# A new order for the first chunk's work, work moved between engines, and blockwise turns on VectorE for three groups

## The chip, the cores and the metric

The kernel runs on one core of a Trainium2 chip. Its engines are TensorE (PE in the rows; PEld is its weight load), VectorE (DVE), ScalarE (ACT), GpSimd (POOL) and SyncE (SP), which here only issues DMAs. The metric is device microseconds of one execution, the median over runs.

## The reference, cut to what matters

Attention comes first: 4 batches, 8 heads of width 64, 768 tokens. Each query sees a local window (distance under 16) and 24 summaries of 32 tokens each: the maximum of the keys and the mean of the values. Then a two-layer network (512 to 2048 to 512, with ELU) runs on all 3072 tokens.

```
k_sum = k.reshape(B, H, nb, block, D).max(axis=3)
v_sum = v.reshape(B, H, nb, block, D).mean(axis=3)
scores_l = scale * np.matmul(q, k.transpose(0, 1, 3, 2))      # kept where |i - j| < 16
scores_s = scale * np.einsum('bhsd,bhnd->bhsn', q, k_sum) + np.log(block)
a = softmax over the concatenation of both
x = matmul(a, concatenate([v, v_sum], axis=2)), heads side by side
h = x @ w_in
g = np.where(h > 0.0, h, np.exp(np.minimum(h, 0.0)) - 1.0)
out = (g @ w_out).astype(np.float32)
```

All inputs are float32 except the weights w_in and w_out, which are float64.

## The kernel before, in words

The network runs over six chunks of 512 tokens. A chunk has 16 hidden slices f of 128. For each slice, layer 1 is 12 matmuls of 128x512 and layer 2 another 12: every operand is split into a high fp32r part and the rest, and three of the four products are kept. That makes 24 matmuls per slice, 384 per chunk and 2304 in all.

The first chunk is special, for it also brings in the weights. Each of the 32 weight blocks (16 of w_in, 16 of w_out) arrives as float64 bits and is converted by five steps: `X` (low bits, POOL), `M` (exponent, ACT, into PSUM), `S` (two joins, DVE), `H` (the high fp32r part, a cast) and `L` (the rest, a subtraction). Also in the first chunk stand the attention of its own 512 tokens (four head pairs, words `sl`, `ss`, `low`, `exp`, `z`, `norm`, `tr`, `ptc`, `val`) and the attention of the second chunk, in groups 0 to 3 of two head pairs each (`gsc`, `glow`, `ge`, `gz`, `gn`, `gtr`, `gpc`, `gval`, `gxh`, `gxl`). ELU is `E` (exponential, ACT) with two more steps, and `G` and `gl` split the result for layer 2. `L1h`, `L1l`, `L2a`, `L2b`, `L2c` are the matmuls; `w`, `kq`, `ve`, `vo`, `q`, `K`, `sk`, `sv`, `vm` issue DMAs on SP; `idle` and `warm` are matmuls on zeros.

The order of all this is written out by hand in the table `FIRST`: a word is a step with its numbers, and each engine executes its own steps strictly in the order of the table. Nothing reorders them later. Chunks 2 to 6 come from a loop (L792 on), whose order a scheduler settles for ACT, DVE and POOL; there the probabilities of a group are turned by `group_blocks`, 16 block transposes on DVE (L580), in place of TensorE's transposes (L199) and a copy out of PSUM (L569).

Buffers matter at a few places. Scores of pair 0 and 3 share two PSUM banks; the turned probabilities of the first chunk all use the two buffers of the bank tag `h`, which layer 1 uses too. The weight tiles lend their space to the first chunk's keys, queries and probabilities, so some weight loads wait for attention steps.

Of the kernel before, what the change touches and what calls it, by code (L numbers as in the profile page):

```python
# [38 lines left out]

FIRST = """  # L40
    kq.2 ve kq.3 vo max.0 sl.0 max.1 ss.0 sl.1 low.0.1 ss.1 idle.2.180 low.0.0 exp.0.1 low.1.0 sums.0 low.1.1
    exp.0.0 sl.2 idle.2.120 w.0 max.2 exp.1.1 z.0 ss.2 w.1 norm.0.1 sums.1 low.2.1 exp.1.0 norm.0.0 tr.0.1
    low.2.0 warm.1.180 q.0 sums.2 ptc.0.1.0 w.2 exp.2.1 z.1 sl.3 max.3 norm.1.0 w.3 exp.2.0 spr.3.0 ss.3
    warm.1.300 norm.1.1 spr.0.0 spr.2.0 low.3.1 w.4 mv.0.2.0 mv.0.0.1 low.3.0 mv.1.0.0 exp.3.1 spr.1.0 mv.1.3.0
    z.2 tr.0.0 warm.1.480 mv.1.1.0 tr.1.1 warm.1.480 ptc.0.0.0 exp.3.0 norm.2.0 sk.0 ptc.1.1.0 norm.2.1 tr.2.0
    q.1 mv.0.1.1 z.3 ptc.2.0.1 X.0 w.5 tr.2.1 mv.1.2.1 X.1 tr.1.0 ptc.2.1.1 val.0 norm.3.0 ptc.1.0.0 M.0 M.1 S.0
    norm.3.1 val.1 mv.0.3.1 xh.0 w.6 X.2 S.1 tr.3.0 xh.1 X.3 tr.3.1 ptc.3.0.1 sk.1 val.2 ptc.3.1.1 xl.0 H.0.1
    w.7 xl.1 val.3 xh.2 H.1.1 X.4 xl.2 L.0 w.8 first.0 xh.3 M.2 xl.3 L.1 first.1 M.3 sk.2 S.2 first.2 w.9
    first.3 S.3 H.2.1 M.4 L1h.1 E.0 L.2 w.10 ts.0 H.3 Y.5 stt.0 L.3 L1l.1 sk.3 S.4 G.0 E.1 gl.0 L2a.0 w.11 M.5
    L2c.0 M.6 Y.6 S.5 H.4 w.12 L2b.0 X.7 ts.1 H.5 L.4 L1h.2 sv.0 M.7 stt.1 L.5 w.13 G.1 S.6 L1l.2 gl.1 S.7 L2a.1  # L50
    H.6 w.14 L2c.1 L.6 H.7 sv.1 L2b.1 E.2 ks.3 L.7 K.2 vl vm.0 vm.1 gsc.0 ts.2 X.8 stt.2 L1h.3 X.9 glow.0.0 G.2
    X.10 glow.0.1 M.8 gl.2 ge.0.0 L1l.3 S.8 q.2 L2a.2 w.15 X.11 E.3 gz.0.0 X.12 L2c.2 H.8 ts.3 w.16 M.9 L.8
    L2b.2 stt.3 M.10 S.9 L1h.4 G.3 sv.2 gn.0.0 ge.0.1 S.10 gl.3 L1l.4 gz.0.1 L2a.3 E.4 gn.0.1 M.11 ts.4 L2c.3
    H.9 stt.4 H.10 L2b.3 L.9 vs.1 G.4 gtr.0.0 L.10 L1h.5 S.11 gl.4 ks.2 H.11 L1l.5 gpc.0.0.1 ks.0 L.11 M.12
    gtr.0.1 ks.1 L2a.4 gpc.0.1.1 X.13 M.13 S.12 L2b.4 X.14 E.5 L2c.4 pm.2 S.13 H.12 pm.3 gval.0 X.15 X.16 ts.5
    H.13 gsc.1 w.17 w.18 sv.3 L.12 stt.5 w.19 G.5 L1h.6 glow.1.0 L.13 gxh.0 glow.1.1 M.14 w.20 gl.5 gxl.0 L1l.6
    M.15 ge.1.0 S.14 w.21 L2a.5 L2b.5 S.15 E.6 gap.6 w.22 H.14 L2c.5 X.17 H.15 L.14 L1h.7 w.23 M.16 gz.1.0
    larger.6 M.17 L.15 S.16 w.24 G.6 L1l.7 ge.1.1 gl.6 L2a.6 S.17 K.3 E.7 gap.7 X.18 L2b.6 H.16 gz.1.1 gn.1.0
    L2c.6 L.16 larger.7 gtr.1.0 vs.2 L1h.8 G.7 q.3 gn.1.1 H.17 vs.0 w.25 gpc.1.0.1 gl.7 vs.3 M.18 L1l.8 S.18
    w.26 gtr.1.1 E.8 X.19 L2a.7 gpc.1.1.1 L.17 ts.8 M.19 w.27 L2b.7 stt.8 X.20 L2c.7 S.19 G.8 X.21 w.28 gval.1  # L60
    gl.8 w.29 gsc.2 gxh.1 X.22 H.18 gxl.1 H.19 L1h.9 L.18 glow.2.0 w.30 M.20 L.19 w.31 ge.2.0 L1l.9 S.20 X.23
    L2a.8 glow.2.1 E.9 X.24 L2b.8 H.20 ts.9 ge.2.1 L.20 L2c.8 stt.9 gz.2.0 mmul G.9 L1h.10 gz.2.1 mact mm gl.9
    M.21 M.22 S.21 L1l.10 gn.2.0 L2a.9 gn.2.1 S.22 M.23 E.10 L2b.9 X.25 H.21 ts.10 X.26 L2c.9 H.22 stt.10 L.21
    gtr.2.0 G.10 L1h.11 gpc.2.0.1 L.22 S.23 M.24 L1l.11 gl.10 S.24 H.23 gtr.2.1 L.23 L2a.10 gpc.2.1.0 H.24
    L2b.10 M.25 L.24 E.11 S.25 L2c.10 X.27 gval.2 K.4 q.4 ts.11 X.28 H.25 stt.11 L.25 gsc.3 G.11 gxh.2 L1h.12
    gl.11 glow.3.1 glow.3.0 ge.3.1 gxl.2 X.29 L1l.12 X.30 M.26 L2a.11 gz.3.1 E.12 gn.3.1 S.26 L2b.11 ge.3.0
    L2c.11 ts.12 H.26 stt.12 L1h.13 M.27 L.26 G.12 S.27 M.28 gl.12 L1l.13 gz.3.0 M.29 L2a.12 S.28 gn.3.0 E.13
    H.27 L2b.12 X.31 ts.13 H.28 L2c.12 L.27 stt.13 gtr.3.0 L.28 L1h.14 S.29 gpc.3.0.1 M.30 G.13 S.30 L1l.14 H.29
    gl.13 gtr.3.1 L2a.13 L.29 gpc.3.1.1 M.31 L2b.13 H.30 S.31 L2c.13 E.14 L.30 gval.3 ts.14 stt.14 gsc.4 gxh.3
    H.31 gxl.3 G.14 L1h.15 L.31 glow.4.0 ge.4.0 gl.14 L1l.15 L2a.14 E.15 ts.15 L2b.14 stt.15 L2c.14 glow.4.1  # L70
    G.15 gl.15 ge.4.1 gz.4.0 gz.4.1 gn.4.0 gn.4.1
# [806 lines left out]
```

## Time and profile before

| | us |
|---|---|
| median of 3 runs | 611.12 (610.88 to 611.23) |
| span of the profiled execution | 1539.6 |
| first matmul of layer 1 in the profiled execution | 55.0 |
| first matmul of the second chunk in the profiled execution | 302.4 |

The profiled execution's span is 2.5 times the time of the runs, and no time beside that span is given for it. So the profile is not a picture of a timed run: it must be read engine by engine, and the prediction says how. Durations stand at the right of each group of rows (busy, mean ns of one); a bracket in a timeline row is the idle time of the engine just before, and what ended it.

### The profile page before, as it was taken

To read this page: it belongs to the slowest core of one execution; us is meant where nothing else is said; L and a number is where in the kernel's file an instruction comes from. 1 tells how busy PE (TensorE), PEld (TensorE's weight loads), DVE (VectorE), ACT (ScalarE), POOL (GpSimd) and SP (SyncE) were. 2 spreads that over 40 slices of the span, in tenths; PEclk is the share of its full clock that TensorE was granted. 3 is DMA by queue.
4 is the path that set the end of the run, shared out by engine and by line. 5 is a ranking of instruction groups with operands and counts; after the bars stand their busy time and mean duration, and the time that the engine had idled before them with its cause. 6 is when DMAs were issued, how large, how long until landed. Compare 5 with 4: busy or idle time off the path is not lost.

```text
span 1539.6 us, 11202 instructions
## 1 busy us (share of the span) xinstructions
PE 1534.8 (100%) x4123; PEld 931.8 (61%) x4123; DVE 364.7 (24%) x1063; ACT 271.8 (18%) x762; POOL 243.2 (16%) x280
## 2 busy tenths in 40 slices
...
GB/s 294 158 109 82 55 51 35 27 28 27 1 53 25 47 71 28 0 26 1 47 47 37 41 7 43 28 1 54 27 0 17 1 0 0 27 0 0 0 0 27
DMA packets 63551, 58.62 MB, mean 38 GB/s; under 512 B 22649, under 2 KB 54905, under 8 KB 63497
## 3 DMA queue, kind: packets, MB, share of 16 engines
q1 hardware_dynamic: 60184, 52.02, 11.0%
...
## 4 chain that ended last, share of the span: by engine, by line
PE 100%; ACT 0%; DVE 0%; issue 0%
PE o L696 38%; PE h L635 37%; PE h L646 7%; PE o L686 7%; PE o_ps L599 3%; PE s L542 3%; PE t_ps L199 1%; PE idle L275 1%; PE s L355 1%; PE o_ps L382 1%; PE h L426 0%; PE vsps L401 0%; PE vsps L512 0%; ACT ots L723 0%; DVE kw L265 0%
## 5 line engine op out<-in xcount | busy, mean ns | idle before, releaser
L635 PE MATMUL h<-xh,w 128*128 128x512 f32 x640 | 472.6, 825 | 0.0
L696 PE MATMUL o<-w,gh 128*128 128x512 f32 x648 | 407.9, 827 | 0.0
L696 PEld LDWEIGHTS o<-w,gh 128*128 128x128 f32 x648 | 225.2, 348 | 160.3 <-issue 160.1
L635 PEld LDWEIGHTS h<-xh,w 128*128 128x128 f32 x640 | 224.1, 350 | 161.2 <-issue 160.1
L676 POOL TENSOR_TENSOR gl<-e,gh 128x512 fp32r<-128x512 f32 x96 | 122.4, 1275 | 944.0 <-ACT gh L671 844.3
L635 PE MATMUL h<-xl,w 128*128 128x512 f32 x320 | 265.9, 831 | 0.0
L655 DVE TENSOR_SCALAR e<-e 128x512 f32<-128x512 f32 x94 | 41.3, 439 | 844.7 <-ACT e L651 844.7
L696 PE MATMUL o<-w,gl 128*128 128x512 f32 x324 | 218.1, 832 | 0.0
L651 ACT ACTIVATE e<-h 128x512 f32<-128x512 f32 x96 | 57.4, 598 | 873.9 <-PE h L635 801.1
L696 PEld LDWEIGHTS o<-w,gl 128*128 128x128 f32 x324 | 115.8, 358 | 73.6 <-issue 71.8
L635 PEld LDWEIGHTS h<-xl,w 128*128 128x128 f32 x320 | 112.3, 351 | 65.5 <-issue 65.5
L580 DVE STREAM_TRANSPOSE pt<-sm 32x256 f32<-32x256 f32 x256 | 111.4, 435 | 4.1
L646 PE MATMUL h<-xh,w 128*128 128x512 f32 x120 | 90.3, 837 | 0.0
L181 ACT ACTIVATE sm<-sm,mx 128x120 f32<-128x120 f32 x160 | 61.5, 388 | 111.5 <-DVE mx L173 111.5
L686 PE MATMUL o<-w,gh 128*128 128x512 f32 x120 | 78.4, 832 | 0.0
L671 ACT CAST gh<-e 128x512 fp32r<-128x512 f32 x96 | 59.5, 620 | 100.9 <-DVE e L666 94.4
L173 DVE CUSTOM_DVE_ANT_0 sm<-s,mask 128x120 f32<-128x120 f32 x160 | 34.2, 279 | 135.3 <-PE s L542 135.3
L666 DVE SCALAR_TENSOR_TENSOR e<-h,e 128x512 f32<-128x512 f32 x94 | 65.0, 692 | 3.2
L190 POOL TENSOR_TENSOR sm<-sm,z 128x480 f32<-128x480 f32 x40 | 38.8, 988 | 139.4 <-DVE z L193 132.1
L646 PEld LDWEIGHTS h<-xh,w 128*128 128x128 f32 x120 | 42.2, 352 | 28.9 <-issue 27.1
L161 POOL TENSOR_TENSOR w<-cv,w 128x512 fp32r<-128x512 f32 x32 | 40.7, 1286 | 119.9 <-ACT w L158 119.7
L686 PEld LDWEIGHTS o<-w,gh 128*128 128x128 f32 x120 | 41.6, 349 | 27.6 <-issue 27.0
...
## 6 DMA issues: line engine op xcount, KB each, us to landing
...
```

Source lines behind the costliest of these rows:

```text
L181: nc.scalar.activation(out=sm[:, t, :], in_=sm[:, t, :], func=AF.Exp, bias=mx[:, t, :], scale=-1.0, accum_out=z[:, t, :])
L542: nc.tensor.matmul(s_of[g, h][half, 2 * i + t // 2, cols], q_t[rows, i, t * QW:(t + 1) * QW], right, start=True, stop=True)
L580: nc.vector.transpose(out=dst[k, :, q], in_=src[q, :, k])
L599: nc.tensor.matmul(o_of[g][cols, i, t * QW:(t + 1) * QW], left, pt[0:KC, h, 2 * i + t // 2, t % 2 * QW:(t % 2 + 1) * QW], start=True, stop ...
L635: nc.tensor.matmul(h_ps, w[:, a, cols], bb[:, cc, :], start=(k == 0), stop=(k == 3 * NCC - 1))
L646: nc.tensor.matmul(h_ps, w[:, lo, cc * P:(cc + 1) * P], bb[:, cc, :], start=(lo, cc, i) == (0, 0, 0), stop=(lo, cc) == (1, NCC - 1))
L651: nc.scalar.activation(out=e, in_=h_ps, func=AF.Exp)
L666: top = nc.vector.scalar_tensor_tensor(out=e, in0=h_ps, scalar=0.0, in1=e, op0=ALU.max, op1=ALU.add)
L671: nc.scalar.copy(out=gh, in_=e)
L676: nc.gpsimd.tensor_tensor(out=gl, in0=e, in1=gs[(c, f)][0].bitcast(F32), op=ALU.subtract)
L686: nc.tensor.matmul(o_acc[0][s], gs[(0, f)][a][:, s * P:(s + 1) * P], w[:, bb, :], start=(f, part) == (0, 0), stop=False)
L696: nc.tensor.matmul(o_acc[c][s], a[:, s * P:(s + 1) * P], w[:, bb, :], start=first and f == 0, stop=last and f == NF - 1)
```

## The change

The table `FIRST` is replaced by another order of nearly the same words. The words also choose other engines or other forms:

| word | before | after |
|---|---|---|
| `L`, rest of a weight | 32 on POOL | 22 on POOL, 10 on DVE |
| `H`, high part of a weight | 29 on ACT, 3 on POOL | 15 on ACT, 17 on POOL |
| `G`, high part of ELU | 16 on ACT | 6 on ACT, 10 on POOL |
| `gl`, rest of ELU | 16 on POOL | 15 on POOL, 1 on DVE |
| ELU after `E` | 14 `ts`+`stt` (DVE, DVE), 2 `gap`+`larger` (ACT, DVE) | 16 `gap`+`larger` |
| `norm` and `gn`, row scaling | 18 on POOL | 12 on POOL, 6 on DVE |
| `mv`, means to value tiles | 4 on POOL, 4 on ACT | 7 on POOL, 1 on ACT |
| `gtr`, four PE transposes each | 8 | 2 (group 0 alone) |
| `gpc`, copy out of PSUM | 7 on ACT, 1 on DVE | 2 on ACT |
| `gb`, four block transposes on DVE each | 0 | 12 (groups 1 to 3) |
| `ptc`, copy out of PSUM | 4 on ACT, 4 on DVE | 5 on ACT, 3 on DVE |
| `idle`, `warm` | 2, 4 | 0, 2 |

`ve` becomes four words, one for each part of its loads, and `tr` takes a bank (seven single banks beside `h`). Words that the table does not use (`zh`, `pb`, `ew`, `rs`, `dm`) are defined as well.

```
+BLOCKS_FROM = 1
 FIRST = """
-    kq.2 ve kq.3 vo max.0 sl.0 max.1 ss.0 sl.1 low.0.1 ss.1 idle.2.180 low.0.0 exp.0.1 low.1.0 sums.0 low.1.1
...
+    max.0 sl.0 ss.0 low.0.1 exp.0.1 max.1 low.0.0 exp.0.0 sl.1 ss.1 ve.2 kq.2 sl.2 low.1.1 exp.1.1 max.2 z.0 ss.2
...
-        def rest(self):
-            nc.gpsimd.tensor_tensor(out=self.w[:, 1, :], in0=self.cv, in1=self.w[:, 0, :].bitcast(F32),
+        def rest(self, engine=nc.gpsimd):
+            engine.tensor_tensor(out=self.w[:, 1, :], in0=self.cv, in1=self.w[:, 0, :].bitcast(F32),
...
-        def trans(p, h):
-            t_of[p, h] = transposes(sms[p][:, h], "h", bufs=2)
+        def norm(p, h, by=0):
+            scale_rows(sms[p][:, h], zs[p][:, h], (nc.gpsimd, nc.vector)[by])
+
+        def trans(p, h, bank=0):
+            t_of[p, h] = transposes(sms[p][:, h], banks[bank], bufs=1 if bank else 2)
...
-            if g >= NP:
+            if g >= BLOCKS_FROM:
                 nc.gpsimd.memset(wide_of[g][:, :, :, KC:P], 0.0)
...
-            "G": lambda n: split_high(0, n, es[n]), "gl": lambda n: split_rest(0, n, es[n]),
+            "G": lambda n, by=0: split_high(0, n, es[n], (nc.scalar.copy, nc.gpsimd.tensor_copy)[by]), "gl": lambda n, by=0: split_rest(0, n, es[n], (nc.gpsimd, nc.vector)[by]),
...
+            "gb": group_blocks, "gval": group_values, "gxh": group_high, "gxl": group_rest,
```

The first place is TensorE's own order in the first attention, from the second pair's summary scores on (`s` scores, `vsps` the sums of values, `t_ps` transposes of `sm_own`, `idle` the matmuls on zeros). Before:

```order
L275 MATMUL idle<-kw_75 128x180 x2
L401 MATMUL vsps<-vxh,mean 32x128 x4
L355 MATMUL s<-kn,qn 64x96 x16
L275 MATMUL idle<-kw_75 128x120 x2
L355 MATMUL s<-ks,qn 128x24 x8
L401 MATMUL vsps<-vxh,mean 32x128 x12
L199 MATMUL t_ps<-ident,sm_own 120x128 x4
L275 MATMUL idle<-kw_75 128x180
L401 MATMUL vsps<-v_own,mean 32x128 x8
L355 MATMUL s<-kn,qn 64x96 x16
L355 MATMUL s<-ks,qn 128x24 x8
L275 MATMUL idle<-kw_75 128x300
```

After:

```order
L360 MATMUL s<-kn,qn 64x96 x16
L360 MATMUL s<-ks,qn 128x24 x8
L424 MATMUL vsps<-vxh,mean 32x128 x4
L277 MATMUL idle<-kw_75 128x344
L360 MATMUL s<-kn,qn 64x96 x16
L360 MATMUL s<-ks,qn 128x24 x8
L201 MATMUL t_ps<-ident,sm_own 120x128 x8
L424 MATMUL vsps<-vxh,mean 32x128 x12
L424 MATMUL vsps<-v_own,mean 32x128 x8
L201 MATMUL t_ps<-ident,sm_own 120x128 x8
L277 MATMUL idle<-kw_75 128x208
```

The scores of all four pairs now stand ahead of every transpose and ahead of most of the value sums, and two matmuls on zeros stand between them in place of six words.

The second place is SP's queue (`raw_w_3` is the raw block of hidden slice 3, `v_own<-vsx` the copy of the value means into the second chunk's own value tiles, `n` blocks of keys for the summaries, `qbd` queries of a group). Before:

```order
L474 DMA kw_73<-in_kT_dram 128x80
L475 DMA vw_77<-in_v_dram 80x128
L334 DMA v_own<-in_v_dram 96x512
L335 DMA v_own<-in_v_dram 80x512
L410 DMA v_own<-vsx 24x2x512 x2
L447 DMA qbd_70<-in_qT_dram 128x2x256
L118 DMA raw_w_8_856<-in_w_in_dram 128x4x128
L118 DMA raw_w_7_870<-in_w_out_dram 128x512
```

After:

```order
L120 DMA raw_w_5_499<-in_w_in_dram 128x4x128
L120 DMA raw_w_2_507<-in_w_in_dram 128x4x128
L120 DMA raw_w_3_527<-in_w_in_dram 128x4x128
L120 DMA raw_w_4_553<-in_w_in_dram 128x4x128
L433 DMA v_own<-vsx 24x2x512
L120 DMA raw_w_1_579<-in_w_out_dram 128x512
L120 DMA raw_w_2_650<-in_w_out_dram 128x512
L120 DMA raw_w_6_666<-in_w_in_dram 128x4x128
```

One of the two `v_own<-vsx` copies, which waits for the value means, now stands ahead of the w_out blocks of slices 1 and 2 and of nearly all later loads.

The third place is DVE where a group of the second chunk is turned; before, around the one copy that DVE makes for group 2 (`pt<-t_ps`), with ELU as L655 and L666:

```order
L655 TENSOR_SCALAR e<-e 128x512
L666 SCALAR_TENSOR_TENSOR e<-h,e 128x512
L149 SCALAR_TENSOR_TENSOR sh<-sh,raw_w_12_1165 128x512
L152 SCALAR_TENSOR_TENSOR cv<-raw_w_12_1165,sh 128x512
L149 SCALAR_TENSOR_TENSOR sh<-sh,raw_w_11_1177 128x512
L152 SCALAR_TENSOR_TENSOR cv<-raw_w_11_1177,sh 128x512
L569 COPY pt<-t_ps 120x512
L149 SCALAR_TENSOR_TENSOR sh<-sh,raw_w_13_1248 128x512
L152 SCALAR_TENSOR_TENSOR cv<-raw_w_13_1248,sh 128x512
L655 TENSOR_SCALAR e<-e 128x512
L666 SCALAR_TENSOR_TENSOR e<-h,e 128x512
```

After, where group 1 is turned (`pt<-sm`), with ELU's last step as L686:

```order
L686 SCALAR_TENSOR_TENSOR e<-e,h 128x512
L603 STREAM_TRANSPOSE pt<-sm 32x8x32 x4
L151 SCALAR_TENSOR_TENSOR sh<-sh,raw_w_9_1009 128x512
L154 SCALAR_TENSOR_TENSOR cv<-raw_w_9_1009,sh 128x512
L151 SCALAR_TENSOR_TENSOR sh<-sh,raw_w_8_866 128x512
L154 SCALAR_TENSOR_TENSOR cv<-raw_w_8_866,sh 128x512
L603 STREAM_TRANSPOSE pt<-sm 32x8x32 x8
L686 SCALAR_TENSOR_TENSOR e<-e,h 128x512
L151 SCALAR_TENSOR_TENSOR sh<-sh,raw_w_10_1076 128x512
L154 SCALAR_TENSOR_TENSOR cv<-raw_w_10_1076,sh 128x512
L686 SCALAR_TENSOR_TENSOR e<-e,h 128x512
L603 STREAM_TRANSPOSE pt<-sm 32x8x32 x4
```

Sixteen block transposes in three runs stand where copies stood, between the joins of the weights.

## Rows read from the trace of the kernel before

**Rows 1.** The page: busy time by engine; the chain that ended last, by line.

```profile
PE 1534.8 (100%) x4123; PEld 931.8 (61%) x4123; DVE 364.7 (24%) x1063; ACT 271.8 (18%) x762; POOL 243.2 (16%) x280
...
PE o L696 38%; PE h L635 37%; PE h L646 7%; PE o L686 7%; PE o_ps L599 3%; PE s L542 3%; PE t_ps L199 1%; PE idle L275 1%; PE s L355 1%; PE o_ps L382 1%; PE h L426 0%; PE vsps L401 0%; PE vsps L512 0%; ACT ots L723 0%; DVE kw L265 0%
```

**Rows 2.** Three stretches: length, busy time and count per engine, clock, DMA share, GB/s.

```profile
0.00:55.10 55.10, 53.98 (x441) 38.56 (x441) 22.51 (x108) 21.81 (x79) 22.19 (x58) 1.00 0.83 293
55.10:302.30 247.20, 247.20 (x745) 150.83 (x746) 77.00 (x186) 77.33 (x191) 82.47 (x85) 1.00 0.20 61
302.30:1539.60 1237.30, 1233.58 (x2939) 742.38 (x2937) 265.14 (x769) 172.66 (x492) 138.53 (x137) 1.00 0.08 22
```

**Rows 3.** The same view, a stretch of the last chunk.

```profile
1300.00:1500.00 200.00, 200.00 (x338) 118.10 (x337) 16.35 (x29) 18.83 (x31) 17.82 (x14) 1.00 0.01 5
```

**Rows 4.** The same view from the second chunk on, scores (L542), then values (L599).

```profile
302.30:1539.60 1237.30, 35.87 (x480) 25.02 (x480) 1.00 0.08 22
...
302.30:1539.60 1237.30, 39.53 (x512) 37.33 (x512) 1.00 0.08 22
```

**Rows 5.** Timeline of the first attention: exponentials that waited.

```profile
15.18 0.40 ACT L181 ACTIVATE sm_own<-sm_own,mean 128x120 f32<-128x120 f32 x1 [1.66 <-DVE mean L173]
...
22.21 0.40 ACT L181 ACTIVATE sm_own<-sm_own,mean 128x120 f32<-128x120 f32 x1 [3.89 <-DVE mean L173]
...
31.52 0.40 ACT L181 ACTIVATE sm_own<-sm_own,mean 128x120 f32<-128x120 f32 x1 [3.25 <-DVE mean L173]
```

**Rows 6.** Chain that ended last: first and last of six pieces of zeros.

```profile
14.01 1.71 PE idle L275 x4
...
37.27 2.16 PE idle L275 x2
```

**Rows 7.** Timeline of SP's queue in the first attention.

```profile
22.33 0.34 SPq L118 DMA_DIRECT2D raw_w<-in_w_out_dram  x1
31.19 0.34 SPq L497 DMA_DIRECT2D n<-in_kT_dram  x1
```

**Rows 8.** Groups by line, whole span: busy, mean ns of one, idle before.

```profile
L676 POOL TENSOR_TENSOR gl<-e,gh 128x512 fp32r<-128x512 f32 x96 | 122.4, 1275 | 944.0 <-ACT gh L671 844.3 <-issue 89.1 <-PE o L696 10.6
...
L580 DVE STREAM_TRANSPOSE pt<-sm 32x256 f32<-32x256 f32 x256 | 111.4, 435 | 4.1
...
L666 DVE SCALAR_TENSOR_TENSOR e<-h,e 128x512 f32<-128x512 f32 x94 | 65.0, 692 | 3.2
...
L655 DVE TENSOR_SCALAR e<-e 128x512 f32<-128x512 f32 x94 | 41.3, 439 | 844.7 <-ACT e L651 844.7
...
L161 POOL TENSOR_TENSOR w<-cv,w 128x512 fp32r<-128x512 f32 x32 | 40.7, 1286 | 119.9 <-ACT w L158 119.7
...
L190 POOL TENSOR_TENSOR sm<-sm,z 128x480 f32<-128x480 f32 x40 | 38.8, 988 | 139.4 <-DVE z L193 132.1 <-DVE z L768 7.2
...
L158 ACT CAST w<-cv 128x512 fp32r<-128x512 f32 x29 | 17.3, 616 | 5.7 <-DVE cv L152 5.7
...
L199 PE MATMUL t_ps<-ident,sm 128*120 128x128 f32 x32 | 11.7, 540 | 0.0
...
L569 ACT COPY pt<-t_ps 120x512 f32<-120x512 f32 x7 | 4.1, 588 | 35.0 <-PE t_ps L199 35.0
...
L391 DVE TENSOR_TENSOR xl<-o_ps,xh 128x512 fp32r<-128x512 f32 x4 | 2.8, 690 | 7.3 <-ACT xh L387 7.3
...
L158 POOL CAST w<-cv 128x512 fp32r<-128x512 f32 x3 | 1.8, 613 | 11.3 <-DVE cv L152 11.3
...
L413 POOL COPY vxl<-vsx 24x512 f32<-24x512 f32 x3 | 1.8, 616 | 3.5 <-DVE vsx L406 3.5
...
L659 ACT ACTIVATE e<-e 128x512 f32<-128x512 f32 x2 | 1.3, 632 | 0.1
```

**Rows 9.** Timeline of DVE and POOL during one slice's ELU.

```profile
134.45 2.69 POOL L161 TENSOR_TENSOR w<-cv,w 128x512 fp32r<-128x512 f32 x2 [8.32 <-ACT w L158]
134.78 1.24 DVE L655 TENSOR_SCALAR e<-e 128x512 f32<-128x512 f32 x1
```

More of the change, by code (lines that the diff above doesn't have):

```diff
@@ L46 @@
[L46 to L65, printed above, removed]
@@ new lines @@
+    tr.2.1.1 w.0 ptc.1.1.1 mv.0.2.0 ptc.2.0.0 z.3 mv.0.0.0 spr.1.0 norm.3.0.1 ptc.2.1.1 norm.3.1.1 M.1 mv.1.0.0
+    val.0 mv.1.2.0 w.2 ptc.1.0.1 val.2 w.9 mv.1.1.1 X.1 S.1 mv.0.1.0 w.3 X.0 M.0 tr.3.1.0 ptc.3.1.1 tr.3.0.0
+    ptc.3.0.1 S.0 w.5 mv.0.3.0 mv.1.3.0 xh.0.0 xl.0 X.2 val.1 xh.1.0 xl.1 w.7 xh.2.0 xl.2 H.0.1 vm.0 L.0.0 val.3 X.3
+    w.4 xh.3.0 xl.3 H.1.0 M.2 L.1.0 S.2 M.3 first.0 H.2.1 first.1 X.9 first.2 first.3 E.0 gap.0 S.3 H.3.1 L.3.0
+    L1h.1 L1l.1 larger.0 Y.5 X.4 M.5 G.0.0 gl.0.0 E.1 L.2.1 S.5 gap.1 larger.1 M.4 w.6 Y.6 L1h.2 L1l.2 w.11 L2a.0
@@ new lines @@
+    gpc.0.1.1 L2b.2 L2a.3 M.13 sv.1 L.11.0 w.14 X.14 gl.4.0 E.5 S.12 sv.0 S.13 H.12.1 gap.5 L2c.3 larger.5 G.5.1
+    w.15 X.15 H.13.0 gval.0 gxh.0 ks.1 pm.2 w.17 X.17 gsc.1 glow.1.1 w.22 L1h.6 L1l.6 glow.1.0 w.16 X.16 w.19 X.19
+    gxl.0 K.2 ge.1.1 gz.1.1 vs.0 gn.1.1.0 L2b.3 L.12.1 M.14 L.13.0 vs.1 w.21 gl.5.0 L2a.4 ge.1.0 M.15 L2b.4 L2c.4
+    L2a.5 L2b.5 L2c.5 S.14 K.3 gz.1.0 H.14.0 L.14.0 M.16 w.25 gn.1.0.0 E.6 gap.6 S.15 H.15.0 L.15.0 L1h.7 S.16
+    H.16.1 w.26 X.25 L.16.0 larger.6 M.17 gb.1.0.4 L1l.7 G.6.0 gl.6.0 L1h.8 M.18 S.17 M.19 w.27 w.28 S.18 H.18.0
@@ L72 @@
+    gl.13.0 L2c.12 E.14 gap.14 larger.14 G.14.1 L1h.15 L1l.15 E.15 gn.3.1.1 L2a.13 M.31 L.28.0 L2b.13 gl.14.0
+    gb.3.0.4 L2c.13 L.30.0 L2a.14 gb.3.4.8 gb.3.8.12 gb.3.12.16 L2b.14 S.31 gval.3 gxh.3 gxl.3 gap.15 larger.15
+    gsc.4 glow.4.1 H.31.0 glow.4.0 L.31.1 G.15.1 gl.15.0 ge.4.1 gz.4.1 ge.4.0 gz.4.0 gn.4.0.1 L2c.14 gn.4.1.0
 """
@@ L187, in reciprocals, with scale_rows @@
         nc.vector.reciprocal(out=z, in_=z)
-    def scale_rows(sm, z):
-        nc.gpsimd.tensor_tensor(out=sm, in0=sm, in1=z.broadcast_to([P, UW, KC]), op=ALU.mult)
+    def scale_rows(sm, z, engine=nc.gpsimd):
+        engine.tensor_tensor(out=sm, in0=sm, in1=z.broadcast_to([P, UW, KC]), op=ALU.mult)
     def normalize(sm, z):
```

81 lines of the change are left out of this document (51 added, 30 removed).

## The prediction

> **What bounds the kernel now.** I read the page first. It shows TensorE busy for all of the span, and a chain of TensorE work alone that ended last [rows 1]. Taken at its word, nothing that the change does on other engines could matter. But the profiled span is 1539.6 us and the runs take 611.12 us, with no time given around the span, so I check the pace before I believe the chain.
>
> In a stretch of the last chunk 338 matmuls start in 200 us, one per 0.592 us [rows 3]. There are 2304 such matmuls of 512 columns, and at that pace they alone take 1364 us, more than twice a whole timed run. So timed runs drive TensorE faster than this profile does: even if they did nothing else, a matmul takes at most 611/2304 = 0.265 us. The granted clock stands at 1.00 in every stretch [rows 2], its level of 2.4 GHz; if one column enters in a cycle, 512 columns take 0.213 us. That is an estimate and my lower end; I take it, because the attention still has to fit into what is left. It is 0.36 of the profile's pace. The durations of DVE, ACT, POOL and of transfers I take from the trace as they are.
>
> The Trainium skill (TensorE: Matmul & The Clock Gate, section "Wait — 56ns, not 53.3ns?") gives 215.7 ns for 512 columns at the full clock. The trace does not agree: its 592 ns is 2.7 times that, at the same granted clock. By that figure the unchanged loop below would take 5 us more and the first chunk 5 us less.
>
> Next the view by stretches [rows 2]. Stage A is the first attention, up to the first matmul of layer 1 at 55.1 us. Stage B is the rest of the first chunk, 247.2 us. The loop of the other five chunks is 1237.3 us and is not changed. In B the engines beside TensorE are busy 77.0 (DVE), 77.3 (ACT) and 82.5 us (POOL), and TensorE's 247.2 us become 88 at 0.36. So in a timed run four engines have nearly equal work in B, each with in-order queues. In the loop DVE has 265 us of work, far below the matmuls' time: there TensorE is the bound, and the loop stays as it is.
>
> What does a timed run spend in A and B? The loop holds 1932 of the 2304 matmuls, 412 us at 0.213. Its attention matmuls take 75.4 us in the profile (35.87 + 39.53) [rows 4], so 27 us at 0.36 and 75 us at the worst. The 3.7 us at the end that TensorE is not busy (1237.3 - 1233.6) stay. That leaves 611 - 412 - 4 - (27 to 75) = 120 to 168 us for A and B. I take 150, a little above the middle, since the attention matmuls run on the same engine at the same clock. For A I take 40 (no engine works over 22.5 us in it, and the profile needs 55.1), so B is 110: its busiest engine is about 80% busy, and 20 us and more go to waits.
>
> **The change, part by part.** Stage A first. The exponentials of the four pairs waited three times for scores: 1.66, 3.89 and 3.25 us, 8.8 together [rows 5]. In that stretch TensorE ran six pieces of zeros [rows 6], while scores of later pairs stood behind them. The new order has all scores ahead of the transposes, and two pieces of zeros. If all three waits go, A ends 8.8 us sooner; if the timed run, with its faster TensorE, does not have these waits, it gains nothing; and two things could even delay it. The first is the added wait on SP: one copy of the value means now stands ahead of nearly all later weight loads, and waits for the fourth spread of the means. Behind it wait the w_out blocks of slices 1 and 2 and then their conversions. But the queue of before stands too, from 22.33 to 31.19 us [rows 7], so I price it at nothing; if that cover is gone, it costs at most the same 8.9 us. The second is the row scaling of pair 3 on DVE, 2 x 0.69 against 2 x 0.99 us, which is a gain. The own banks of the turns, the loads of `ve` in four words and the dropped zeros have no price of their own: they take away waits of TensorE and SP in A, and stand in the same term. I take -6 for A, between 0 and -8.8 and nearer to the rows, with +8.9 as the bad end.
>
> Stage B, engine by engine, from the rows of single operations [rows 8]. DVE: 14 steps `ts` go (14 x 0.439 = -6.1), and `larger` takes the place of `stt` at equal size. Seventeen subtractions and scalings come, 10 `L`, 1 `gl`, 6 `norm` and `gn`. With two operands in SBUF they have no row; the nearest are 0.439 (one operand, below) and 0.692 (with PSUM, above), and I take 0.690 of the same operation at L391: +11.7 (7.5 at the lower end). The 48 block transposes bring 48 x 0.435 = +20.9, two copies go (-1.4). Sum +25.1; 2.1 of it (three `norm`) lies in A, and one of the copies too, so B has +23.7: 77.0 becomes 100.7 us.
>
> POOL: 10 `L` (-12.9), 1 `gl` (-1.3), 6 scalings (-5.9) go; 24 casts come, 14 `H` and 10 `G`, at 0.613 (+14.7), and three `mv` at 0.616 (+1.8). Without the parts in A it is -2.5: 80.0 us. ACT: 14 `gap` at 0.632 (+8.8), 24 casts go at 0.616 (-14.8), five copies out of PSUM go at 0.588 (-2.9): -8.9, so 68.4 us. TensorE: 24 transposes go, 24/32 of 11.7 us = -8.8 in the profile, -3.2 at 0.36: 85 us. They also leave two copies out of each group's path from scaling to values, but 16 block transposes, 7.0 us, take their place on it.
>
> So B's work leaves three engines and piles up on DVE: 101 us, against 88 for the busiest before. B cannot be shorter than that. At 110 us before, DVE would have to be busy 92% of the time for no loss at all. The order helps it: joins and transposes stand in runs, layer 1 runs up to two slices ahead of layer 2, and the ELU chain no longer asks DVE twice. I take DVE busy 93% and B 108, -2. The ends are 101 (never waiting, -9) and 101/0.8 = 126 (as busy as the busiest engine before, +16).
>
> One rule speaks against moving work between these two engines. While POOL ran two `L` from 134.45 to 137.14 us, a DVE `ts` beside it took 1.24 us in place of 0.43 [rows 9], so 0.8 us was lost to the neighbour. The Trainium skill (SBUF — State Buffer, section "Who interferes with whom") says why: a DVE operation in a two-port mode, or with two operands in SBUF, and a GpSimd operation that reads SBUF block each other for a whole instruction. The row agrees for the first kind; no run here shows the second. By the rule the 17 new operations on DVE can each lose up to 0.8 us; but 14 `ts`, which lose it now, go, so the sum would move by 3 x 0.8 = 2.4 us at most. If the second kind did not lose it, the change would gain up to 14 x 0.8 = 11 us of DVE time. I leave both out of the sum.
>
> The sum is -6 in A and -2 in B: 603 us.
>
> **The rivals.** (1) DVE becomes the wall, and the kernel is slower. In B its queue is in order, with runs of up to 16 transposes (7.0 us) ahead of the joins that the next weights wait for and of the ELU steps that the next layer 2 waits for. For it speaks that DVE's work in B grows by a third; against it, that 20 us of waits are there now to be filled. With A at -6 it decides from B = 116, DVE busy 87%. At 80% B is 126 and the time 611 - 6 + 16 = 621; about the middle, 617, is what I expect of this case.
>
> (2) The waits of B go nearly all. A stage of four nearly equal engines at 110 us has room for it; then B is DVE's 101 and the loss of A's waits comes on top: 611 - 6 - 9 = 596, and 590 if the first chunk of before was nearer to the 168 us end. Against it: no engine of before came close to that.
>
> (3) Nothing is left of it: A ends sooner, but B starts with weights that are not there, for the loads keep their pace (the transfers are busy 0.83 of A [rows 2]), and B ends when DVE's fixed work ends. Then the time is 611, within 0.2%.
>
> **How the numbers follow.** About 0.2% of 611 us, 1.2 us, is what a measurement of this kernel can tell from no change. I give the forecast (600 to 609) 0.38, rival 1 0.31, rival 2 0.19 and rival 3 0.12. The forecast and rival 2 are faster: 0.57. Rival 3 is the same: 0.12. Rival 1 is slower: 0.31. The range, 590 to 618, takes in both ends of rival 2 and the likelier half of rival 1; beyond it lie DVE under 83% in B and a bound of TensorE alone. Cases of both signs hold most of the chance, and the likeliest one's own range is 600 to 609.
>
> **What the changed profile would show.** The profiled execution will again be paced by TensorE, so I would look at the other engines' work, not at the chain. Step A is right if the exponentials' waits [rows 5] shrink to under 3 us together and layer 1 starts well before 55 us. The counts are right if DVE's busy time in the first chunk is near 99.5 + 25 = 124.6 us, POOL's near 101 and ACT's near 89; a two-operand subtraction on DVE that takes over 0.8 us on the mean would show the block by POOL. If waits of ELU or of casts on DVE grow where a run of transposes stands, rival 1 is on its way. The forecast is wrong if a timed run is over 611, and its reason is wrong if A did not become shorter.

## The result, and the profile after

The changed kernel takes 618.93 us (median of 4 runs, 617.56 to 620.14), against 611.10 us for the kernel before on the same chip: ratio 1.0124, 95% interval 1.0101 to 1.0146. It is slower by 8 us. The forecast was 603.0 us with a range of 590 to 618, so the direction was wrong and the time lies just outside the range, on the side of rival 1. The profiled execution is the 620.00 us one, at a mean granted clock of 0.989 like the 620.14 one; the other two, 617.56 and 617.86, had 0.994, so the loss of the profiled one lies at the upper end.

The page of the changed kernel has a span of 618.3 us: this profile ran at the pace of the timed runs, unlike the 1539.6 us of the profile before. Its busy times, the granted clock in 40 slices, and its chain by engine and by line (compare [rows 1]):

```profile
PE 602.7 (97%) x4087; PEld 491.1 (79%) x4087; DVE 395.6 (64%) x1111; ACT 258.2 (42%) x746; POOL 249.8 (40%) x293
...
PEclk8699999999999999999999999999999999999999
...
PE 82%; DVE 8%; POOL 4%; DMA 2%; issue 2%; SPq 1%; ACT 1%; ACTq 0%; DVEq 0%; POOLq 0%
PE h L658 36%; PE o L719 36%; DVE pt L603 3%; PE s L565 3%; PE o_ps L622 3%; POOL w L163 1%; DVE cv L154 1%; DMA raw_w<-in_w_in_dram 1%; PE s L360 1%; DVE sh L151 1%; POOL raw_w L139 1%; PE o_ps L405 1%; POOL w L160 1%; DMA vw<-in_v_dram 1%; PE h L669 0%
```

Two things are to be seen. In the second slice (15 to 31 us) TensorE ran at 0.6 of its full clock. And the chain passes through DVE for 8% of the span and through POOL for 4%; what it was before, at this pace, experiment 1 shows.

The three stretches, cut as in [rows 2] (columns: length; PE, PEld, DVE, ACT, POOL busy with counts; granted clock; DMA share; GB/s):

```profile
0.00:33.50 33.50, 27.82 (x429) 22.11 (x429) 22.52 (x108) 20.49 (x78) 18.23 (x53) 0.80 0.90 306
33.50:140.30 106.80, 100.80 (x736) 79.16 (x735) 99.46 (x232) 67.68 (x171) 90.11 (x105) 1.00 0.61 190
140.30:618.30 478.00, 474.08 (x2927) 389.83 (x2925) 273.61 (x773) 170.06 (x499) 141.41 (x137) 1.00 0.20 59
```

Stage A is 33.5 us (I had 34) and stage B 106.8 (I had 108). DVE's work in B is 99.5 us (I had 100.7), 93% of the stage as I had it. So the lengths of the changed first chunk came out as forecast, A's by luck: I had 40 less 6, and it was 30.0 (experiment 1) and 3.5 more. What I did not know was the first chunk of the kernel before.

### The profile page after: what moved, and what is told of

The parts are those of the page before. It is cut to its first block, busy times and chain, and to the rows that moved or that the text cites. A ratio compares the mean times of both kernels' runs of the same rounds, so it can differ in the third digit from the quotient of the medians.

```text
span 618.3 us, 11168 instructions
## 1 busy us (share of the span) xinstructions
PE 602.7 (97%) x4087; PEld 491.1 (79%) x4087; DVE 395.6 (64%) x1111; ACT 258.2 (42%) x746; POOL 249.8 (40%) x293
## 4 chain that ended last, share of the span: by engine, by line
PE 82%; DVE 8%; POOL 4%; DMA 2%; issue 2%; SPq 1%; ACT 1%; ACTq 0%; DVEq 0%; POOLq 0%
PE h L658 36%; PE o L719 36%; DVE pt L603 3%; PE s L565 3%; PE o_ps L622 3%; POOL w L163 1%; DVE cv L154 1%; DMA raw_w<-in_w_in_dram 1%; PE s L360 1%; DVE sh L151 1%; POOL raw_w L139 1%; PE o_ps L405 1%; POOL w L160 1%; DMA vw<-in_v_dram 1%; PE h L669 0%
## 5 line engine op out<-in xcount | busy, mean ns | idle before, releaser
L658 PE MATMUL h<-xh,w 128*128 128x512 f32 x640 | 212.2, 393 | 0.0
L719 PE MATMUL o<-w,gh 128*128 128x512 f32 x648 | 163.0, 389 | 0.0
L719 PEld LDWEIGHTS o<-w,gh 128*128 128x128 f32 x648 | 121.6, 188 | 25.3
L658 PEld LDWEIGHTS h<-xh,w 128*128 128x128 f32 x640 | 120.1, 188 | 26.0
L603 DVE STREAM_TRANSPOSE pt<-sm 32x256 f32<-32x256 f32 x304 | 132.5, 436 | 6.6 <-POOL sm L192 1.5
L658 PE MATMUL h<-xl,w 128*128 128x512 f32 x320 | 124.6, 389 | 0.0
L719 PE MATMUL o<-w,gl 128*128 128x512 f32 x324 | 89.5, 389 | 0.0
L719 PEld LDWEIGHTS o<-w,gl 128*128 128x128 f32 x324 | 60.8, 188 | 12.6
L658 PEld LDWEIGHTS h<-xl,w 128*128 128x128 f32 x320 | 60.1, 188 | 11.9
L175 DVE CUSTOM_DVE_ANT_0 sm<-s,mask 128x120 f32<-128x120 f32 x160 | 34.1, 278 | 24.3 <-PE s L565 23.7
L669 PE MATMUL h<-xh,w 128*128 128x512 f32 x120 | 39.3, 395 | 1.3 <-DVE e L686 1.2
L709 PE MATMUL o<-w,gh 128*128 128x512 f32 x120 | 32.1, 397 | 1.0 <-POOL w L163 0.8
L163 POOL TENSOR_TENSOR w<-cv,w 128x512 fp32r<-128x512 f32 x22 | 29.8, 1357 | 1.5 <-ACT w L160 0.6
L183 ACT ACTIVATION_READ_ACCUMULATOR sm<-sm,mx 128x1 f32 x160 | 30.1, 188 | 0.0
```

What stands on the lines that cost most here:

```text
L163: engine.tensor_tensor(out=self.w[:, 1, :], in0=self.cv, in1=self.w[:, 0, :].bitcast(F32), op=ALU.subtract)
L183: nc.scalar.activation(out=sm[:, t, :], in_=sm[:, t, :], func=AF.Exp, bias=mx[:, t, :], scale=-1.0, accum_out=z[:, t, :])
L603: nc.vector.transpose(out=dst[k, :, q], in_=src[q, :, k])
L658: nc.tensor.matmul(h_ps, w[:, a, cols], bb[:, cc, :], start=(k == 0), stop=(k == 3 * NCC - 1))
L669: nc.tensor.matmul(h_ps, w[:, lo, cc * P:(cc + 1) * P], bb[:, cc, :], start=(lo, cc, i) == (0, 0, 0), stop=(lo, cc) == (1, NCC - 1))
L719: nc.tensor.matmul(o_acc[c][s], a[:, s * P:(s + 1) * P], w[:, bb, :], start=first and f == 0, stop=last and f == NF - 1)
```

## The experiments

The stages of a run are cut as above; only the rows that a verdict rests on are shown. "TensorE held up" is worked out from the starts of the matmuls in B: what lies beyond 0.26 us between one start and the next, summed.

**1. The kernel before, again** (nothing edited).

> The kernel before, unchanged, profiled once more, for a trace at the pace of the timed runs. If the loop of the last five chunks lasts the 478.0 us that it lasts in the changed kernel's trace, the first chunk takes 611.1 - 1.7 - 478.0 = 131 us, against 140.3 in the changed kernel. Theory 1 (VectorE's work is the wall of the second stage): stage A about 38 us, stage B about 93, VectorE busy about 78 us in B (under 85%). Theory 2 (late weight loads in the changed kernel): the same lengths, but the chain of before holds no piece of SP's queue or of a transfer in B, where the changed kernel's has one from 47 to 71 us. Theory 3 (the clock): the granted clock in A is 0.95 or more here, against 0.80 in the changed kernel.

It took 611.85 us, and this time the profile's span was 610.1 us. Its chain by engine, its stretches, and one stretch in the last chunk that holds nothing but full matmuls:

```profile
PE 92%; DMA 5%; ACT 1%; POOL 1%; SPq 1%; DVE 0%; issue 0%; ACTq 0%; DVEq 0%
```

```profile
0.00:30.00 30.00, 26.41 (x441) 19.43 (x441) 22.05 (x108) 21.23 (x79) 19.46 (x56) 1.00 0.98 343
30.00:129.30 99.30, 97.98 (x746) 78.88 (x746) 77.92 (x187) 76.08 (x191) 86.69 (x88) 1.00 0.65 208
129.30:610.10 480.80, 476.88 (x2939) 392.31 (x2938) 272.99 (x769) 169.51 (x492) 141.99 (x138) 1.00 0.20 57
550.00:600.00 50.00, 50.00 (x222) 41.41 (x221) 11.29 (x20) 11.55 (x19) 11.87 (x10) 1.00 0.00 0
```

The first chunk of before is 129.3 us long, not 150, and TensorE is busy 98.0 of B's 99.3 us: B was bound by TensorE and had no 20 us of waits to fill. A full matmul takes 50.0/222 = 0.225 us.

The two spans differ by 8.2 us. A is 3.5 longer. B is 7.5 longer, but 12 matmuls of layer 2 that stood behind the cut now stand ahead of it: B holds 180 of them instead of 168, and the loop is 2.8 us shorter for it. That leaves +4.7 in B, and 3.5 + 4.7 = 8.2. By the starts, TensorE was held up 3.4 us in B before and 8.5 us after; its turns fell from 2.85 us (32 matmuls) to 0.71 (8), and the scores and values of the second chunk's attention, counted up to 0.26 us a start, rose from 9.8 to 11.5. Together: 5.1 + 1.7 - 2.1 = 4.7.

The matmuls in B that waited, and for whom; first after, then before (us in total, times, longest):

```profile
PE s L565 <- DVE cv L154: 1.7, 2, 1.1
PE o_ps L622 <- DVE pt L603: 1.5, 3, 0.6
PE h L669 <- DVE e L686: 1.2, 1, 1.2
PE o L709 <- POOL w L163: 0.8, 2, 0.5
```

```profile
PE o L686 <- POOL w L161: 0.7, 1, 0.7
PE o L686 <- POOL gl L676: 0.5, 1, 0.5
```

After, matmuls wait for DVE's join (`cv`), for its block turns (`pt`) and for its ELU step (`e`), 4.4 us together; before, no matmul waits for DVE. The chain says the same: DVE has 8% of it after and none before.

**2. Half of one table, half of the other.** The order of one kernel up to the first matmul of layer 1, and then the words of the other:

```
after_A_before_B:  words of after up to first.0, then before's from first.0 (those already done left out)
before_A_after_B:  words of before up to first.0, then after's from first.0 (the same)
```

> The changed table up to the first matmul of layer 1, and from there the table of before (its engines, TensorE's turns, no blocks). Theory 1: A as in the changed kernel (33.5 us), B as before, about 93, so 606 to 608 us if the new A is some 5 us shorter than the old one. Theory 2 (late loads come with the new table's SP order of B): also about 606, since SP's order in B is the old one. Theory 3 (A's colder clock costs what its order gains): 611.

> The other half: the table of before up to the first matmul of layer 1, then the changed one (blocks, changed engines, changed SP order). Theory 1: A about 38 us, B about 107, time 621 to 625 us, slower than the changed kernel. Theory 3 (the loss lies in A's clock): 611 or less.

New A with old B took 615.1 us (ratio 1.0060, 1.0040 to 1.0080), old A with new B 620.54 (1.0142, 1.0120 to 1.0163). A and B of each:

```profile
0.00:32.98 32.98, 27.10 (x429) 20.89 (x429) 22.80 (x108) 20.48 (x78) 18.20 (x53) 0.84 0.93 309
32.98:132.66 99.68, 98.16 (x750) 78.83 (x746) 77.95 (x188) 76.60 (x193) 87.68 (x90) 1.00 0.64 208
```

```profile
0.00:29.20 29.20, 25.92 (x441) 19.12 (x441) 21.89 (x108) 21.21 (x79) 19.44 (x56) 1.00 0.97 344
29.20:141.07 111.87, 102.76 (x735) 80.34 (x734) 98.30 (x231) 67.31 (x169) 88.89 (x103) 0.98 0.59 184
```

Each half costs by itself: the new A 3 us (with the clock at 0.84), the new B more. The old B behind the new A keeps its 99.7 us, so the later weight loads of the new A cost B next to nothing. Behind the old A the new B is even 111.9: the seam has a wait of some 3.2 us for a weight's cast at 35.0 us, and behind it the clock fell (0.98 on the mean of B), which cost 1.6 us more, so this run overstates B's own price.

**3. The clock in stage A.** One kernel puts zero matmuls into the new table, the other takes them out of the old one:

```
after + zeros:     - ... sl.1 ss.1 ...          + ... sl.1 idle.4.180 ss.1 ...
                   - ... sl.2 low.1.1 ...       + ... sl.2 idle.4.180 low.1.1 ...
before - zeros:    - idle.2.180  idle.2.120  warm.1.180  warm.1.300  warm.1.480  warm.1.480
```

> The changed kernel with eight matmuls on a zeroed tile (180 columns, results never read) put back where its TensorE waits for the key sums: four behind each of the second and third pair's plain scores. Theory of the clock (the first stage is 3.5 us longer because the granted clock stands at half from about 11 to 25 us, after TensorE was busy only 3.3 of 5 us, and scores, mean sums and turns run on the path meanwhile): granted clock back near 1.00, first stage 29.5 to 31, total 615 to 617. Rival, the order (VectorE's and the load queue's order set the 33.5 us): clock up, first stage still 33 or longer, total 619 to 620.

> The kernel before without the matmuls on zeros in its table (two idle and four warm words); all else as it was. Theory of the clock: the granted clock falls to half in the first stage as it does in the changed kernel, first stage 32 to 34 instead of 30.0, total 613 to 616. Rival, the order: the matmuls on zeros only fill waits, first stage 29.5 to 30.5, total 610 to 612.

The changed kernel with zeros took 615.9 us (1.0070, 1.0054 to 1.0087; A is 30.73 at clock 0.94), the kernel before without them 613.62 (1.0034, 1.0020 to 1.0048; A is 32.35 at clock 0.79). Both went as the theory of the clock has it, and in both B stayed as it was (the profiled execution with zeros is the longest of its four, 617.3 us):

```profile
0.00:30.73 30.73, 27.04 (x444) 21.79 (x444) 23.00 (x108) 20.10 (x78) 19.54 (x54) 0.94 0.99 337
30.73:137.56 106.83, 100.75 (x738) 79.15 (x734) 99.49 (x232) 67.67 (x171) 88.83 (x104) 1.00 0.63 190
```

```profile
0.00:32.35 32.35, 26.87 (x424) 21.23 (x424) 22.62 (x108) 21.56 (x79) 20.56 (x57) 0.79 0.99 347
32.35:131.77 99.42, 97.77 (x749) 78.94 (x746) 78.34 (x187) 76.12 (x191) 85.74 (x87) 1.00 0.62 199
```

Stage A of the changed kernel, 5 us at a time, shows it directly:

```profile
5.00:10.00 5.00, 3.26 (x113) 2.75 (x112) 3.93 (x21) 2.33 (x12) 2.01 (x16) 1.00 1.04 370
10.00:15.00 5.00, 3.95 (x61) 3.27 (x60) 3.81 (x28) 4.73 (x25) 1.93 (x2) 0.65 1.05 387
15.00:20.00 5.00, 5.00 (x54) 3.81 (x53) 2.49 (x18) 2.87 (x16) 1.93 (x2) 0.50 1.08 370
20.00:25.00 5.00, 5.00 (x54) 4.15 (x53) 3.00 (x18) 2.72 (x15) 1.59 (x2) 0.50 0.59 173
```

TensorE waited for key sums (busy 3.26 of 5 us; in the kernel before it was busy all of the same 5), then the granted clock fell to 0.50, which is 1.2 GHz, for some 13.5 us (added up from the shares in the rows), and in these TensorE was busy nearly all the time. The same 32 plain scores at either level, on the timeline of that kernel:

```profile
10.12 0.89 PE L360 MATMUL s<-kn,qn 64*64 64x96 f32 x32
...
15.92 1.56 PE L360 MATMUL s<-kn,qn 64*64 64x96 f32 x32
```

Where the zeros kept the clock at 1.00 through all of A (three runs of experiments 5 and 6 below, which start with this same stage), the new A took 29.05 us, as long as the old one (28.97 to 30.0 in its runs); in the three others with the same zeros the clock was 0.94 and A 30.6 to 30.8. So the new order of A costs nothing and gains nothing; the dropped zeros cost some 3 us (33.5 - 30.73 = 2.8 in the new A, 32.35 - 30.0 = 2.4 in the old one). With the zeros the changed kernel is still 0.7% slower, some 4.3 us, which is close to B's loss of 4.7.

Why neither order is shorter than 29 us is in part seen: in the kernel before the chain of the first 34 us runs mostly on transfers, which are busy 0.98 of A, and they are as busy (0.98) in the new A when its clock stays at 1.00.

```profile
by line: DMA raw_w<-in_w_in_dram 27.4%; DMA raw_w<-in_w_out_dram 21.4%; DMA vxh<-in_v_dram 20.7%; DMA qn<-in_qT_dram 12.3%; SPq L447 9.8%; SPq L118 2.2%; DVE sh L149 2.1%; DVE cv L152 2.1%; issue 0.8%; DVEq L152 0.1%
```

No run with lighter loads in A was made, so that the transfers bound the new A too is not shown.

**4. One part of B at a time.** The turns alone moved in the old table; the casts alone moved back in the new one; the turns alone moved back in the new one:

```
before + blocks:      - gtr.1.0 ... gpc.1.0.1 ... gtr.1.1             ... gpc.1.1.1
                      + ...                       gb.1.0.4 gb.1.4.8   ... gb.1.8.12 gb.1.12.16   (groups 2, 3 too)
after, casts on ACT:  - H.0.1  G.2.1  ...   + H.0.0  G.2.0  ...       (27 words)
after, PE turns:      - gn.1.1.0 ... gb.1.0.4 ...   + gn.1.1.0 gtr.1.1 gpc.1.1.1 ...   (groups 2, 3 too)
```

> The kernel before, its order kept, with only the turns of groups 1 to 3 moved from TensorE to VectorE blocks (24 transposes and 6 evictions off, 12 block turns on). Its first chunk ends at 129.3 us with TensorE busy 98.0 of 99.3 in the second stage. Theory 1 (the turns on VectorE alone make the new second stage longer, whatever the order): VectorE goes from 77.9 to 96 or more, matmuls wait for it, second stage 103 to 107, total 615 to 619. Theory 2 (the longer stage comes from the other moves, the casts on POOL and the order; TensorE is the wall and loses 24 transposes of some 0.05 to 0.1 us): second stage 96 to 99, total 608 to 611.

> The changed kernel, order and blocks kept, with the 28 casts of weights and activations that its table gives to POOL back on ScalarE (which then has some 85 of 107 us work in the second stage, POOL some 72 instead of 90). Theory 1 (VectorE, 99.5 of 106.8 us busy, sets the second stage): 106 to 108, total 618 to 620. Theory 2 (the matmuls wait for POOL, whose queue carries the casts ahead of the remainders): the waits for POOL's remainders go, second stage 101 to 104, total 613 to 616.

> The changed kernel, but groups 1 to 3 are turned on TensorE and copied out of PSUM by ScalarE again, as before; each turn stands right behind its scaling where its bank is free. All else, with the loads and the engines of the other words, is as changed. Theory 1 (VectorE is the wall of B): VectorE's work in B falls from 99.5 to about 78.6 us, B from 106.8 to 95 or less, time 606 to 610 us. Theory 2 (late loads): the same chain of loads remains, B stays within 2 us, time 616 to 620 us.

All three came out worse than anything expected: 630.81 us (1.0316, 1.0298 to 1.0334), 635.8 (1.0392, 1.0366 to 1.0417) and 624.8 (1.0228, 1.0204 to 1.0252). Stage B of each, in this order:

```profile
28.97:148.89 119.92, 104.64 (x727) 83.95 (x726) 96.83 (x235) 73.84 (x187) 86.64 (x91) 0.91 0.56 178
```

```profile
31.64:154.18 122.54, 107.18 (x733) 83.10 (x734) 100.53 (x239) 81.51 (x200) 73.79 (x80) 0.94 0.53 168
```

```profile
32.92:147.24 114.32, 104.83 (x761) 83.47 (x758) 78.35 (x179) 70.62 (x176) 89.17 (x101) 0.97 0.56 177
```

In none is an engine beside TensorE the wall: DVE is busy 96.8 of 119.9, 100.5 of 122.5 and 78.4 of 114.3 us. What stretches B, as far as the waits show it, is a word that reaches the head of its queue too early. With the blocks in the old table the values wait for them three times for 4 to 5 us, since they stand right ahead of them; with the casts back on ScalarE, POOL waits 26.4 us in 11 pieces for them; with TensorE's turns close behind their scaling, ScalarE's copies wait 16.4 us for the turns, and DVE's joins 14.1 us for ScalarE. The rows in this order:

```profile
PEld o_ps L598 <- DVE pt L579: 15.1, 6, 5.0
```

```profile
POOL w L163 <- ACT w L160: 26.4, 11, 4.7
...
PEld h L669 <- ACT w L160: 8.6, 5, 3.3
```

```profile
ACT pt L592 <- PE t_ps L201: 16.4, 4, 4.9
DVE sh L151 <- ACT sh L147: 14.1, 6, 4.8
```

The waits cost twice, for the clock fell behind the longest of them: it is 0.91, 0.94 and 0.97 on the mean of B, and TensorE is busy 104.6, 107.2 and 104.8 us in place of 98.0 (old table) and 100.8 (new), though the first has 24 turns less and the third 24 more, some 2 us.

So a part of this change can't be priced alone in this way: the table is written for its own mix of engines.

**5. Less work, same order.** To price an engine's load without moving a word, I cut work and left the table as it is. The first kernel leaves out three quarters of the block turns of groups 1 to 3, the second the low bits of three quarters of the columns from the fifth weight on, the third both. The base is the changed kernel with zeros (615.9 us, B 106.8).

```
blocks/4:   - nc.vector.transpose(out=dst[k, :, q], in_=src[q, :, k])
            + n = 2 if 1 <= g <= 3 else 8
            + nc.vector.transpose(out=dst[k, 0:n, q], in_=src[q, 0:n, k])
low bits/4: - nc.gpsimd.tensor_scalar(out=self.lo, ...)
            + n = WC // 4 if self.j > 3 else WC
            + nc.gpsimd.tensor_scalar(out=self.lo[:, 0:n], ...)
```

> The changed kernel with the eight zero matmuls of the run before (615.9 us, second stage 106.8, TensorE held up 8.6 us in it), and the block turns of groups 1 to 3 cut to a quarter: each of the 48 turns 2 of 8 blocks, and the matmuls behind read those two blocks again, so that three quarters of these groups' turned scores are left out. Takes some 12 to 14 us of VectorE's work off the second stage, everything else and the order as they were. Theory D (matmuls wait for VectorE: its turns and, queued behind them, its joins and ELUs): TensorE's waits fall to 4 to 5 us, second stage 102 to 104, total 611 to 613. Theory P (they wait for POOL, 89 us busy with casts added to its queue): second stage 106 to 107, total 615 to 617.

> The same base (615.9 us), VectorE's work as it was, and POOL's low-bit words from the fifth weight on cut to a quarter of their columns: the joins read that quarter four times, so that the low bits of the other columns are left out. Takes some 11 to 13 us off POOL's 89. Theory P: TensorE's waits fall to 4 to 5 us, second stage 102 to 104, total 611 to 613. Theory D: second stage 105.5 to 107, total 614.5 to 617.

> Both cuts at once, on the same base (615.9 us). Theories D and P alike, if one of them is the cause: no better than the better of the two single cuts, 611 to 613. If TensorE's 8.6 us of waits come from both engines alike: second stage 99 to 102, total 608 to 611. If neither (the order of the words itself sets them): second stage 105 to 107, total 614 to 617.

Times: 610.55 us (0.9999, 0.9981 to 1.0017), 616.05 (1.0066, 1.0041 to 1.0092), 608.79 (0.9950, 0.9932 to 0.9968). Stage B of the three:

```profile
29.05:130.74 101.69, 98.92 (x737) 78.86 (x734) 89.81 (x227) 67.58 (x170) 89.69 (x104) 1.00 0.66 206
```

```profile
30.79:136.54 105.75, 100.58 (x737) 80.92 (x734) 99.48 (x232) 67.63 (x171) 80.01 (x104) 0.98 0.61 193
```

```profile
30.63:129.11 98.48, 97.41 (x737) 79.31 (x734) 88.16 (x227) 67.51 (x170) 79.89 (x103) 1.00 0.66 207
```

With 9.7 us less on DVE, B is 5.1 us shorter; with 8.8 us less on POOL, 1.1; with both, 8.3. The 1.1 is too low, for the clock was 0.98 in that B. Executions with a mean granted clock of 0.999 or 1.000 took 615.6 to 616.1 us (base), 610.4 to 610.6, 613.2 (one execution) and 607.3 to 607.6: by their medians 5.2 us for DVE's load, some 2.4 for POOL's and 8.2 for both. So in this order the block turns hold TensorE up, as theory D has it; POOL's load counts about half as much, and the two nearly add up. With both cut, TensorE is busy 97.4 of B's 98.5 us.

**6. Turns back on TensorE, later.** Experiments 4 and 5 seemed to disagree: a quarter of the blocks helps, no blocks at all hurt. So the turns went back to TensorE again, on the base with zeros, but not right behind their scaling:

```
late:   - S.15 H.15.0 ... gb.1.0.4 ... gl.6.0 ...   + S.15 gtr.1.1 gpc.1.1.1 H.15.0 ... gl.6.0 gtr.1.0 gpc.1.0.0 ...
last:   - S.18 H.18.0 ... S.19 w.20 ...             + S.18 H.18.0 gtr.1.0 gpc.1.0.0 ... S.19 gtr.1.1 gpc.1.1.1 w.20 ...
```

> The changed kernel with the eight zero matmuls (615.9 us, second stage 106.8), and the turns of groups 1 to 3 back on TensorE with their copies half on VectorE and half on ScalarE, this time put 12 words and more behind the scaling that they read, where a bank is free, and not right behind it as in the run that took 624.8 us. Theory D (VectorE's 48 block turns hold up the matmuls; the 624.8 us came from where the turns stood): VectorE some 82 instead of 99.5 us, TensorE 2 us more of its own work, waits 3 to 5 us instead of 8.6, second stage 101 to 104, total 609.5 to 613. Rival (this order suits only blocks: any TensorE turn in it waits for POOL's scaling or holds up ScalarE's queue): second stage 107 or longer, total 616 to 625.

> The same with the TensorE turns as late as their banks allow, the second of groups 1 and 2 shortly ahead of the matmuls that read them. Theory D with the place of the words as a cost of its own: waits of 0.5 to 1 us for the copies in groups 1 to 3, second stage 102 to 106, total 610.5 to 615. Rival as in the run beside it: 616 to 625.

They took 616.74 us (1.0086, 1.0064 to 1.0107) and 620.27 (1.0144, 1.0125 to 1.0164). Stage B:

```profile
29.05:136.18 107.13, 102.01 (x761) 81.43 (x758) 80.65 (x182) 69.31 (x173) 89.38 (x101) 1.00 0.62 195
```

```profile
29.06:138.88 109.82, 102.50 (x761) 81.60 (x758) 79.96 (x182) 69.18 (x173) 89.33 (x101) 1.00 0.61 192
```

The place is worth up to 7 us: B is 114.3, 109.8 and 107.1 for three places of the turns (in the first all copies were ScalarE's and the clock was 0.97, in the others half of the copies and 1.00). But even the best place gives the 106.8 us that the blocks give, with DVE 19 us lighter: lengths and times are those of the rival, not of theory D. The waits have changed hands, not gone. The rival put them down to POOL's scaling or ScalarE's queue; in the run with late turns TensorE waits for DVE's ELU step (2.2 us) and, ahead of a turn, for a join of DVE (1.2):

```profile
PE h L669 <- DVE e L686: 2.2, 2, 1.2
PE t_ps L201 <- DVE cv L154: 1.2, 1, 1.2
```

Which words of the new order would have to move for B to come under 102 us with all its work is open.

**7. A shorter wait in the kernel before.** TensorE's longest wait in the old B is 0.86 us, ahead of the first layer 2, which needs the first ELU:

```
- ts.0 ... stt.0      + gap.0 ... larger.0
```

> The kernel before, whole, with the first activation's ELU by ScalarE and one VectorE step (the other of its two forms) instead of two VectorE steps: TensorE's longest wait in its second stage is 0.86 us for this activation at 35.7 us. If that wait is on the path (TensorE is the wall of this stage): 0.5 to 0.9 us less, 610 to 611. If not: 611 to 612, the same.

It took 610.80 us against 611.07, ratio 1.0006 (0.9990 to 1.0022): not to be told from no change. The wait fell by 0.4 us and B from 99.3 to 99.1. None of the kernels with all the work beats the kernel before.

## Why the prediction was wrong

- **The step that failed is the price of a matmul.** I put 512 columns at 0.213 us and so the loop at 412 us for its 1932 large matmuls. They take 0.225 us in a steady stretch and 0.229 on the mean of the loop (0.016 us more each, 30 us in all; the rest of the loop came out at 39 us where I had 49). I then gave what was left, 150 us, to the first chunk. It was 129.3, inside my bounds of 120 to 168 but near the low end. Part of the ground was no ground: I read a granted clock of 1.00 off [rows 2], but the trace of that profile holds no record of the granted clock (its page has no row PEclk), so the 1.00 there says nothing.
- **From it came the 20 us of waits in B that were not there.** I scaled TensorE's work in B to 88 us of 110 and read the rest as waits that a better order could fill. It was 98.0 of 99.3. A B of 108 us was a gain of 2 by my sum; the 106.8 that came was a loss of 4.7.
- **The ceiling that I overlooked.** Even if the new table had left TensorE no wait in B, the gain in B would have been the 3.4 us of waits and the 2.1 us of turns.
- **Stage A: the sign was wrong.** Of the 8.8 us of waits of the exponentials [rows 5] only 0.8 is there at the timed pace, so there was next to nothing to win (the row below; after the change it is 2.3; the first exponential, which the 8.8 leave out, waits 4.41 us in both). And the zeros [rows 6], which I took for an obstacle ahead of the scores, kept the clock at 1.00. I gave their removal no price; it cost some 3 us of the 3.5. SP's added wait, which I priced at nothing with 8.9 us as the bad end, was 4.2 us in the changed kernel, while earlier loads kept the transfers busy, and cost nothing that shows: with the new A the old B is 99.7 us.

```profile
18.84 0.40 ACT L181 ACTIVATE sm_own<-sm_own,mean 128x120 f32<-128x120 f32 x1 [0.79 <-DVE mean L173]
```

- **The counts held for DVE and ACT, not for POOL.** In the first chunk DVE is busy 122.0 us (I had 124.6), ACT 88.2 (89, though my own terms add up to 90.2) and POOL 108.3 (101). DVE's work in B rose by 21.5 us (I had 23.7). The steps `ts` that went had taken 0.652 us each in B, not 0.439, and the `L` on DVE 0.921, not 0.690. TensorE's 24 turns were worth 2.1 us (I had 3.2). POOL's work in B did not fall to 80.0 but is 90.1 (before, at this pace, 86.7); some 2.5 us of that is slower operations (26 casts at 658 to 677 ns in place of 613, 22 subtractions at 1357 in place of 1310), the rest was not taken apart.
- **Rival 1 named the mechanism of B** with its place: joins and ELU steps behind the block turns. Its point of decision was wrong: it had B at 116, and with A no shorter it was 99.3 + 2.8 = 102.1, DVE busy 97% of it. The experiment with a quarter of the blocks shows 5.1 us for this mechanism, as much as B's loss of 4.7, while the late turns show that taking the blocks away again does not win it back. That DVE's queue holds the matmuls up is shown; that an order with all the work exists in which it does not is open.
